# Value products of the third and fourth chunk in one run, and the scores around that run in another order

## Chip, core and metric

One NeuronCore of a Trainium2 chip runs the whole program. The metric is the device time of one execution in microseconds (us), as the median of several runs. A profile of one execution gives every instruction's start and duration.

## What is computed

A gate mixes sliding-window attention with a SwiGLU feed-forward network, for S = 2048 rows of D = 512 in fp32 (H = 32 heads of 16, window W = 256, F = 1792):

```python
def _A_ref(x, wqkv, wo):
    q, k, v = ...                       # x @ wqkv, H heads of 16
    scores = einsum("bhqd,bhkd->bhqk", q, k) * 16 ** -0.5
    p = softmax(where(0 <= q - k < 256, scores, -1e9))
    return einsum("bhqk,bhkd->bhqd", p, v)... @ wo
def _B_ref(x, w_gate, w_up, w_down):
    return (silu(x @ w_gate) * (x @ w_up)) @ w_down
g = sigmoid((x * gate_w).sum(-1, keepdims=True))
return g * _A_ref(x, ...) + (1 - g) * _B_ref(x, ...)
```

## The kernel before, in words

Products that need fp32 accuracy are made of two reduced-precision halves: each operand is split into a high and a low part (`split`), and three products are added.

The heads are worked on in eight groups of four (`g` = 0 to 7); the keys and queries in 16 blocks of 128 rows; the output of a group in four chunks of 512 queries (`c` = 0 to 3). The program has a start (projections of the first groups and all values), a main loop, and a last part (`with ExitStack() as B`: output projection and down projection).

The main loop runs over 128 slots `t` (and one more), 16 for each group; `i` is `t` modulo 16. The order of the instructions on every engine is that in which the Python code issues them; nothing is reordered by a planner. A slot has four turns (`hd`). In each turn TensorE gets:

- one score product of `stage1` for the next group (L263), into one of two `ps1` buffers of PSUM. VectorE (DVE) adds the mask and takes the row maximum from it (L265);
- one score product of `stage2` for this group (L305), into one of two `ps2` buffers. ScalarE (ACT) takes its exponential into a tile `pt` of SBUF (L307), and GpSimd (POOL) zeroes what lies outside the window (L309, L312). The two scores of a turn use the two halves of the array's rows (`j` is 0 or 1) and run at the same time;
- three pairs of matmuls of a projection or of the feed-forward network (`lanes`, L215), one matmul of a pair on each half of the rows, into `pa` or `pb` (two buffers each).

In the last group (slots from `g7` = 112) there is no `stage1`; the `stage2` scores come in pairs in turns 0 and 2, one pair in `ps2` and the other in `ps1`.

Value products (`av`, L329) multiply exponentials by values: 48 products for a chunk (32 for chunk 0), in 64x32 pieces of the array, each of them two instructions in fp32. They add into one `pp` buffer (`pb`, or `pa` for the very last chunk) and one `ps2` buffer. `values` issues them behind turn 1: chunks 0 and 1 of a group in one run in slot `i` = 8, chunk 2 in `i` = 12, chunk 3 in `i` = 0 of the next group. Then `finish` runs for each chunk, its steps spread over later turns by `times`: ACT copies the `ps2` part, DVE adds the other part, transposes (`across`), divides, transposes (`back`), and POOL sends the result to memory.

`unit` spreads the L215 work: four slots make one unit, and ACT copies its results out of `pa` and `pb` in slots that `later` names; `late` moves the two copies of the second half up to the end of the unit's last slot. `put_max` and `get_max` send the row maxima by memory into the query tiles; `load_v` fetches the values of four blocks into one of three `vg` buffers. After the loop, what is still in `FIN` and `AT` is issued. The last part begins with 24 products (L736), then the down projection (L83 to L85), whose operands come from ACT (L739, L65) and DVE (L740, L68).

Before all this, ten small matmuls on an identity tile (L175) keep TensorE busy while the first inputs arrive.

Of the kernel before, what the change touches and what calls it, by code (L numbers as in the profile page):

```python
# [9 lines left out]
F32 = mybir.dt.float32  # L10
F32R = mybir.dt.float32r
AF = mybir.ActivationFunctionType
ALU = mybir.AluOpType
# [3 lines left out]
P = 128  # L17
# [16 lines left out]
def gated_mix(ctx, tc, xT, xn, w01, wqk, wv, wo, wgu, wd, gw, out):  # L34
# [9 lines left out]

    ident = const.tile([P, P], F32, name="ident")
    make_identity(nc, ident)
    vd = dram.tile([G, P, NB, VW], F32, name="vd")
# [121 lines left out]
    with ExitStack() as A:  # L169
        sm = A.enter_context(tc.tile_pool(name="sm", bufs=2))  # L170


        warm = pp.tile([P, CH], F32, name="pa")
        for _ in range(5):
            nc.tensor.matmul(warm[:, :P], ident, ident, start=True, stop=True)  # L175

        mask = sm.tile([P, 3 * P], F32, name="mask", bufs=1)

        def kept():
            return sm.tile([P, CH], F32, name="ev", bufs=EV)  # L180

# [69 lines left out]
        def stage1(g, qb):  # L251

            hf, b = divmod(qb, NB // 2)
            if b == 0:
                MX[g, hf] = sm.tile([P, 4, NB // 2], F32, name="mx")
            q0, k0 = qb * P, max(0, qb - 2) * P
# [15 lines left out]
        def put_max(g, hf):  # L272
            mt = sm.tile([P, 32], F32, name="mt")
# [12 lines left out]
        VG, PT, AV = {}, {}, {}  # L286
        RC = sm.tile([P, CH // 32], F32, name="rc", bufs=1)

        def load_v(n):

            VG[n] = sm.tile([P, 4, VW], F32, name="vg", bufs=3)
            nc.sync.dma_start(VG[n], vd[n // 4, :, n % 4 * 4:n % 4 * 4 + 4])

        def stage2(g, kb):
# [4 lines left out]
            for hd in (1, 0, 3, 2):  # L299
                pr, j = divmod(hd, 2)  # L300
                r = slice(64 * j, 64 * j + 64)
                if j:
                    pt = PT[g, kb, pr] = ptp.tile([P, 2, 3 * P], F32, name="pt")
# [197 lines left out]
        for c in range(2, NCH):  # L501
            run(proj(1, c, pp, "pb"))
        stack(1, 1)
        for n in range(3):
            load_v(n)
        vp.close()
        osb = A.enter_context(tc.tile_pool(name="osb", bufs=3))
        ptp = A.enter_context(tc.tile_pool(name="ptp", bufs=17))

# [8 lines left out]
        def unit(key, t):  # L518
# [81 lines left out]
        def gate_done():  # L600
            nc.scalar.activation(gate, gate, AF.Exp, scale=-1.0)
            nc.vector.tensor_scalar(gate, gate, 1.0, None, op0=ALU.add)
            nc.vector.reciprocal(gate, gate)
            nc.vector.tensor_scalar(igate, gate, -1.0, 1.0, op0=ALU.mult, op1=ALU.add)
        later(g7 + NB - 1, 3, gate_done)

        FIN, tops = {}, [(0, 1)]
        LOADS = {9: 3, 13: 4, 17: 5, 18: 6}  # L610

        def values(t):

            ag, m = divmod(t - 8, NB)
            if m == 0:
                cs, times = (0, 1), [((0, 1),) * 2 + ((0, 3), (2, 0), (2, 3)), ((0, 1), (0, 2), (1, 1), (3, 2), (4, 1))]
            else:
                cs, times = (1 + m // 4,), [((0, 1), (0, 2), (1, 1), (2, 1), (3, 1))]
            for c in cs:
                av(ag, c)  # L620
            for k, steps in enumerate(zip(*(finish(ag, c) for c in cs))):
                for todo, ts in zip(steps, times):
                    dt, hd = ts[k]
                    if (dt, hd) == (0, 1):
                        todo()
                    else:
                        FIN.setdefault((t + dt, hd), []).append(todo)
        for t in range(G * NB + 1):
# [4 lines left out]
            s1 = stage1(g + 1, i) if t < g7 else iter(())  # L633
            s2 = stage2(g, i) if t < G * NB else iter(())
            for hd in range(4):
                run(s1, 1)
                if t < g7:
                    run(s2, 1)
                elif hd % 2 == 0:
                    run(s2, 2)  # L640
                run(turns[part], 3)
                for f in FIN.pop((t, hd), ()):
                    f()
                for f in AT.pop((t, hd), ()):
                    f()
                if hd == 1 and part == 0:
                    while tops:
                        top = tops.pop()
                        put_max(*top)
                        later(t + 1, 1, lambda top=top: get_max(*top))  # L650
# [10 lines left out]
        for key in sorted(AT):  # L661
            for f in AT[key]:
                f()

    with ExitStack() as B:
# [178 lines left out]
```

## Time and profile before

| what | value |
|---|---|
| time, median of 3 runs | 819.94 us (819.65 to 819.96) |
| the profiled execution's own time | 819.19 us |
| its span, first to last instruction | 817.2 us |
| TensorE (PE) busy | 810.5 us, 99% of the span |
| DVE / ACT / POOL busy | 513.5 / 452.9 / 343.4 us |

In the profile PE is a matmul, PEld a weight load, and L12 is line 12 of the kernel. `pb<-pt,vg` says that the tile `pb` is written from `pt` and `vg`; `ps` stands for the buffers `ps1` and `ps2`. The profiled execution is 0.75 us under the median of the runs.

### The profile page before, as it was taken

The page shows a single profiled execution, that of the slowest core. Times are in us where ns is not written, and L with a number is a line of the kernel's source. Part 1 is how long each engine was busy: PE and PEld are TensorE (multiplying, and loading weights), DVE is VectorE, ACT ScalarE, POOL GpSimd, SP SyncE. Part 2 cuts the span into 40 slices and gives each one's busy share as a digit, 9 for nine tenths or more (in the row PEclk, how much of TensorE's full clock was granted, in tenths as well). Part 3 has the DMA queues.
Part 4 walks back from the last instruction along what each step waited for, and adds up shares of the span by engine and source line. Part 5 has one row for each costly group of instructions (what it writes and reads, how often), then busy time and mean ns, then how long its engine had stood idle before and what let it go on. Part 6 is the DMA issues. An engine that isn't in the chain of part 4 may idle for free.

```text
span 817.2 us, 21557 instructions
## 1 busy us (share of the span) xinstructions
PE 810.5 (99%) x8306; PEld 681.7 (83%) x8306; DVE 513.5 (63%) x1422; ACT 452.9 (55%) x940; POOL 343.4 (42%) x635
## 2 busy tenths in 40 slices
PE   9999999999999999999999999999999999999997
PEld 5788988888888888898888888888788888888886
DVE  5596667667668667677677678854467443443542
ACT  6422656656666666676666665666666423343341
POOL 5812546645546555654554654465610111011020
PEclk9999999999999999999999999999999999999999
DMA  8484615625634642652652565565689444463731
GB/s 295 113 262 145 182 68 165 195 76 151 184 109 118 189 147 85 175 174 70 187 179 89 161 185 165 161 217 171 216 302 322 156 139 141 159 203 103 221 89 52
DMA packets 70326, 133.27 MB, mean 163 GB/s; under 512 B 14288, under 2 KB 19024, under 8 KB 70224
## 3 DMA queue, kind: packets, MB, share of 16 engines
q1 hardware_dynamic: 65936, 116.95, 46.3%
q0 software_dynamic: 4288, 14.95, 5.1%
q8 instruction: 65, 1.06, 0.6%
q14 instruction: 37, 0.30, 0.1%
HBM read 61.08 MB, written 45.61 MB: 131 GB/s over the span
## 4 chain that ended last, share of the span: by engine, by line
PE 95%; DMA 2%; POOL 1%; SPq 1%; DVE 0%; issue 0%; ACT 0%; ACTq 0%
PE pb L215 24%; PE pa L215 24%; PE ps L85 6%; PE ps L83 6%; PE ps L84 6%; PE ps L263 6%; PE pb L329 6%; PE ps L305 5%; PE ps L329 3%; PE pb L85 2%; PE pb L83 2%; PE pb L84 2%; PE pa L736 1%; PE pb L736 1%; PE pb L195 1%; DMA k<-xT 1%
## 5 line engine op out<-in xcount | busy, mean ns | idle before, releaser
L265 DVE CUSTOM_DVE_ANT_0 ps<-ps,mask 128x384 f32<-128x384 f32 (+2 forms) x512 | 273.1, 540 | 119.0 <-PE ps L263 68.7
L307 ACT ACTIVATE pt<-ps 128x384 f32<-128x384 f32 (+2 forms) x512 | 239.4, 476 | 117.9 <-PE ps L305 57.5
L309 POOL TENSOR_SCALAR_AFFINE_SELECT pt<-pt 128x256 f32<-128x256 f32 x256 | 109.1, 426 | 222.3 <-ACT pt L307 209.3
L305 PE MATMUL ps<-q,k 64*128 64x384 f32 (+2 forms) x512 | 159.7, 326 | 0.0
L263 PE MATMUL ps<-k,q 63*128 63x384 f32 (+2 forms) x512 | 157.9, 328 | 0.0
L215 PE MATMUL pb<-xhi,wh 64*128 64x512 f32 x512 | 110.9, 393 | 0.0
L215 PE MATMUL pa<-xhi,wh 64*128 64x512 f32 x512 | 110.7, 393 | 0.0
L215 PE MATMUL pb<-xhi,wl 64*128 64x512 f32 x512 | 109.8, 392 | 0.0
L215 PE MATMUL pb<-xlo,wh 64*128 64x512 f32 x512 | 109.8, 391 | 0.0
L215 PE MATMUL pa<-xlo,wh 64*128 64x512 f32 x512 | 109.3, 391 | 0.0
L215 PE MATMUL pa<-xhi,wl 64*128 64x512 f32 x512 | 109.1, 391 | 0.0
L263 PEld LDWEIGHTS ps<-k,q 63*128 63x128 f32 x512 | 88.8, 185 | 14.2 <-issue 4.0
L312 POOL TENSOR_SCALAR_AFFINE_SELECT pt<-pt 128x256 f32<-128x256 f32 x224 | 96.9, 433 | 0.0
L305 PEld LDWEIGHTS ps<-q,k 64*128 64x128 f32 x512 | 91.4, 185 | 5.9 <-issue 0.6
L329 PE MATMUL ps<-pt,vg 64*32 64x320 f32 (+4 forms) x1408 | 75.1, 346 | 0.0
L740 DVE TENSOR_TENSOR sg<-got,sg 128x512 f32<-128x512 f32 x50 | 43.7, 874 | 48.1 <-ACT sg L739 48.1
L329 PE MATMUL pb<-pt,vg 64*32 64x320 f32 (+3 forms) x1360 | 72.3, 350 | 0.1
L265 DVE DVE_READ_ACCUMULATOR2_ANT mx<- 128x1 f32 x512 | 72.2, 141 | 0.0
L329 PEld LDWEIGHTS pb<-pt,vg 64*32 64x32 f32 x1360 | 48.8, 106 | 20.8 <-ACT pt L307 5.8
L215 PEld LDWEIGHTS pb<-xhi,wh 64*128 64x128 f32 x512 | 55.8, 185 | 8.1 <-ACT ev L529 0.2
L215 PEld LDWEIGHTS pa<-xhi,wh 64*128 64x128 f32 x512 | 55.7, 185 | 7.5 <-ACT ev L529 0.6
L215 PEld LDWEIGHTS pb<-xhi,wl 64*128 64x128 f32 x512 | 55.8, 184 | 7.1
(163 smaller groups left out, 1555.6 us busy)
## 6 DMA issues: line engine op xcount, KB each, us to landing
raws<-ev SPq DMA_DIRECT2D x100, 256.0 KB
got<-raws SPq DMA_DIRECT2D x100, 256.0 KB
od<-on POOLq DMA_DIRECT2D x32, 256.0 KB, 2.6
raw<-wgu SPq DMA_DIRECT2D x28, 256.0 KB
q<-xhi SPq DMA_DIRECT2D x56, 128.0 KB
k<-xhi SPq DMA_DIRECT2D x56, 128.0 KB
vd<-vs POOLq DMA_DIRECT2D x8, 672.0 KB, 6.0
vg<-vd SPq DMA_DIRECT2D x32, 168.0 KB
```

What stands on the lines that cost most here:

```text
L83: nc.tensor.matmul(ps, lh, rh, start=start and i == 0, stop=False)
L84: nc.tensor.matmul(ps, lh, rl, start=False, stop=False)
L85: nc.tensor.matmul(ps, ll, rh, start=False, stop=stop and i == n - 1)
L215: mm = nc.tensor.matmul(ps[me], w[r], x[r], start=not second and i == 0, stop=bool(second) and i == n - 1)
L263: nc.tensor.matmul(ps[:, :n], QT[g % 2][pr][r, q0:q0 + P], KT[g % 2][pr][r, k0:k0 + n], start=True, stop=True)
L265: mx = nc.vector.tensor_tensor_reduce(out=ps[:, :n], in0=ps[:, :n], in1=mask[:, 3 * P - n:], scale=1.0, scalar=NEG, op0=ALU.add, op1=ALU.m ...
L305: nc.tensor.matmul(ps[:, :n], KT[g % 2][pr][r, k0:k0 + P], QT[g % 2][pr][r, k0:k0 + n], start=True, stop=True)
L307: BEHIND.append(nc.scalar.activation(pt[:, j, :n], ps[:, :n], AF.Exp, scale=SCALE))
L309: nc.gpsimd.affine_select(out=pt[:, :, :P], in_=pt[:, :, :P], pattern=[[0, 2], [1, P]], compare_op=ALU.is_ge, fill=0.0, base=0, channel_mu ...
L312: nc.gpsimd.affine_select(out=pt[:, :, 2 * P:], in_=pt[:, :, 2 * P:], pattern=[[0, 2], [-1, P]], compare_op=ALU.is_ge, fill=0.0, base=-1, ...
L329: nc.tensor.matmul(AV[g, c][h][32 * j:32 * j + 32, q0 - c * CH:q1 - c * CH], VG[4 * g + kb // 4][o, kb % 4, 17 * j:17 * j + 32], PT[g, kb, ...
L740: nc.vector.tensor_tensor(out=sg, in0=gu[1], in1=sg, op=ALU.mult)
```

## The change

Chunks 2 and 3 are multiplied together in slot `i` = 0 of the next group, so that a group has two runs of value products in place of three. For that, the exponentials of blocks 6 to 15 have to be kept until then: there are 18 `pt` tiles in place of 17, and block 15 (128 queries wide) uses the free columns of block 14's tiles. The first `stage2` score of the next group can be issued only behind the run. So in slots with `i` = 0 (but not in slot 0) the scores are issued in another order: two of `stage1` behind turn 0's L215 work, none in turn 1, one of `stage1` and one of `stage2` at the head of turns 2 and 3, and two of `stage2` behind turn 3's L215 work. The copies of the unit that ends in `i` = 15 are now `late`. The steps of `finish`, `load_v`, `put_max`, the computing of `igate` and some memory are moved. The warm-up uses a tile zeroed by DVE.

```diff
-    ident = const.tile([P, P], F32, name="ident")
-    make_identity(nc, ident)
...
-        warm = pp.tile([P, CH], F32, name="pa")
-        for _ in range(5):
-            nc.tensor.matmul(warm[:, :P], ident, ident, start=True, stop=True)
+        warm, zero = pp.tile([P, CH], F32, name="pa"), kept()[:, :P]
+        nc.vector.memset(zero, 0.0)
+        for _ in range(5):
+            nc.tensor.matmul(warm[:, :P], zero, zero, start=True, stop=True)
...
-        RC = sm.tile([P, CH // 32], F32, name="rc", bufs=1)
+        RC = igate
...
-                if j:
+                if kb == NB - 1:
+                    pt = PT[g, kb, pr] = PT[g, kb - 1, pr][:, :, 2 * P:]
+                elif j:
                     pt = PT[g, kb, pr] = ptp.tile([P, 2, 3 * P], F32, name="pt")
...
-        ptp = A.enter_context(tc.tile_pool(name="ptp", bufs=17))
+        ptp = A.enter_context(tc.tile_pool(name="ptp", bufs=18))
...
-                    late = hf and (t >= g7 or t % NB == 4)
+                    late = hf and (t >= g7 or t % 8 == 4)
...
-        LOADS = {9: 3, 13: 4, 17: 5, 18: 6}
+        LOADS = {9: 3, 17: 4, 18: 5, 19: 6}
         def values(t):
-            ag, m = divmod(t - 8, NB)
-            if m == 0:
-                cs, times = (0, 1), [((0, 1),) * 2 + ((0, 3), (2, 0), (2, 3)), ((0, 1), (0, 2), (1, 1), (3, 2), (4, 1))]
-            else:
-                cs, times = (1 + m // 4,), [((0, 1), (0, 2), (1, 1), (2, 1), (3, 1))]
+            ag, hf = divmod(t // 8 - 1, 2)
+            cs = 2 * hf, 2 * hf + 1
+            times = ((0, 1), (0, 1), (0, 3), (2, 1), (3, 1)), ((0, 1), (0, 2), (1, 1), (5, 1), (6, 1))
...
+            while part == 0 and tops:
+                top = tops.pop()
+                put_max(*top)
+                later(t + 1, 1, lambda top=top: get_max(*top))
             for hd in range(4):
-                run(s1, 1)
-                if t < g7:
+                if t and i == 0:
+                    if hd > 1:
+                        run(s1, 1)
+                        run(s2, 1)
+                elif t < g7:
+                    run(s1, 1)
                     run(s2, 1)
                 elif hd % 2 == 0:
                     run(s2, 2)
                 run(turns[part], 3)
+                if t and i == 0 and hd in (0, 3):
+                    run((s1, s1, s1, s2)[hd], 2)
...
-                if hd == 1 and part == 0:
-                    while tops:
-                        ...
-                    if t > 4 and i != 4:
-                        values(t)
+                if hd == 1 and t and t % 8 == 0:
+                    values(t)
...
-            m = (t - 3) % NB + 3
+            m = (t - 4) % NB + 4
...
+        nc.vector.tensor_scalar(igate, gate, -1.0, 1.0, op0=ALU.mult, op1=ALU.add)
...
-        wop.tile([P, 1536], F32, name="rest")
+        wop.tile([P, 448], F32, name="rest")
...
-    nc = bacc.Bacc("TRN2", target_bir_lowering=False, num_devices=1, dynamic_dma_scratch_size=4096)
+    nc = bacc.Bacc("TRN2", target_bir_lowering=False, num_devices=1, dynamic_dma_scratch_size=2048)
```

The line that computed `igate` in `gate_done` is gone from there, and the tiles `mx` and `mt` have one buffer in place of two.

## Rows read from the trace of the kernel before

**Rows 1.** The page: busy time of the engines, and the last chain by engine.

```profile
PE 810.5 (99%) x8306; PEld 681.7 (83%) x8306; DVE 513.5 (63%) x1422; ACT 452.9 (55%) x940; POOL 343.4 (42%) x635
...
PE 95%; DMA 2%; POOL 1%; SPq 1%; DVE 0%; issue 0%; ACT 0%; ACTq 0%
```

**Rows 2.** PE's waits: total us, times, longest us.

```profile
PE pa L175 <- POOL ident masks.py:199: 1.4, 1, 1.4
...
PE pa L195 <- DMA q<-xT: 0.2, 1, 0.2
```

**Rows 3.** Windows between the pair runs of neighbouring groups: length, then busy us.

```profile
108.82:173.79 64.97, 64.97 (x865) 55.39 (x864) 46.08 (x153) 42.21 (x93) 35.41 (x72) 1.00 0.46 143
...
433.70:498.67 64.97, 64.97 (x866) 55.40 (x864) 46.08 (x153) 42.20 (x93) 35.46 (x72) 1.00 0.53 159
```

**Rows 4.** Timeline of PE, one regular turn: start us, duration us.

```profile
380.01 0.33 PE L305 MATMUL ps<-q,k 64*128 64x384 f32 x1
380.18 0.39 PE L215 MATMUL pa<-xhi,wh 64*128 64x512 f32 x2
...
380.88 0.33 PE L305 MATMUL ps<-q,k 64*128 64x384 f32 x1
```

**Rows 5.** Timeline of ACT, the exponentials of that turn's and the next turn's score.

```profile
380.47 0.49 ACT L307 ACTIVATE pt<-ps 128x384 f32<-128x384 f32 x1 [0.43 <-PE ps L305]
381.29 0.49 ACT L307 ACTIVATE pt<-ps 128x384 f32<-128x384 f32 x1 [0.32 <-PE ps L263]
```

**Rows 6.** Timeline of PE around a run of one chunk (`i` = 12).

```profile
386.27 0.40 PE L215 MATMUL pa<-xhi,wh 64*128 64x512 f32 x2
...
387.07 0.45 PE L329 MATMUL pb<-pt,vg 64*32 64x320 f32 x1
...
389.04 0.27 PE L329 MATMUL pb<-pt,vg 64*32 64x128 f32 x1
...
389.55 0.44 PE L305 MATMUL ps<-q,k 64*128 64x384 f32 x1
389.83 0.40 PE L215 MATMUL pa<-xhi,wh 64*128 64x512 f32 x2
```

**Rows 7.** Timeline of PE in a run of chunks 0 and 1.

```profile
370.16 0.31 PE L329 MATMUL ps<-pt,vg 64*32 64x64 f32 x8
...
370.45 0.45 PE L329 MATMUL ps<-pt,vg 64*32 64x320 f32 x1
...
372.94 0.44 PE L305 MATMUL ps<-q,k 64*128 64x384 f32 x1
```

**Rows 8.** Timeline of ACT, its first copy behind that run.

```profile
373.04 0.59 ACT L342 COPY on<-ps 128x512 f32<-128x512 f32 x1 [1.72 <-PE ps L329]
```

**Rows 9.** Timeline of ACT in slot 112.

```profile
532.71 0.59 ACT L529 COPY ev<-pb 128x512 f32<-128x512 f32 x1
```

**Rows 10.** Timeline of PE in slot 112.

```profile
532.84 0.41 PE L215 MATMUL pa<-xhi,wl 64*128 64x512 f32 x2
533.36 0.45 PE L329 MATMUL pb<-pt,vg 64*32 64x320 f32 x1
```

**Rows 11.** Timeline of PE, the last run of the loop (slot 128).

```profile
592.29 0.45 PE L329 MATMUL pa<-pt,vg 64*32 64x320 f32 x1
```

**Rows 12.** Timeline of ACT at the end of the loop.

```profile
592.41 1.07 ACT L529 COPY ev<-pb 128x512 f32<-128x512 f32 x2 [0.36 <-PE pb L215]
```

**Rows 13.** Timeline of DVE in the first steps of the last part.

```profile
596.97 0.69 DVE L346 TENSOR_TENSOR on<-pa,on 128x512 f32<-128x512 f32 x1 [4.22 <-ACT on L342]
...
601.54 0.70 DVE L352 STREAM_TRANSPOSE on<-on 128x512 f32<-128x512 f32 x1
...
603.66 0.65 DVE L740 TENSOR_TENSOR sg<-pb,sg 128x512 f32<-128x512 f32 x1
...
605.00 0.69 DVE L68 TENSOR_TENSOR hl<-sg,hh 128x512 fp32r<-128x512 f32 x1
```

**Rows 14.** Timeline of PE where the last part first uses that product.

```profile
606.24 0.39 PE L85 MATMUL ps<-k,hl 128*128 128x512 f32 x1
```

More of the change, by code (lines that the diff above doesn't have):

```diff
@@ L7 @@
 from concourse._compat import with_exitstack
-from concourse.masks import make_identity
 F32 = mybir.dt.float32
@@ L170, in gated_mix @@
         sm = A.enter_context(tc.tile_pool(name="sm", bufs=2))
-        warm = pp.tile([P, CH], F32, name="pa")
-        for _ in range(5):
-            nc.tensor.matmul(warm[:, :P], ident, ident, start=True, stop=True)
-        mask = sm.tile([P, 3 * P], F32, name="mask", bufs=1)
         def kept():
             return sm.tile([P, CH], F32, name="ev", bufs=EV)
+        warm, zero = pp.tile([P, CH], F32, name="pa"), kept()[:, :P]
+        nc.vector.memset(zero, 0.0)
+        for _ in range(5):
+            nc.tensor.matmul(warm[:, :P], zero, zero, start=True, stop=True)
+        mask = sm.tile([P, 3 * P], F32, name="mask", bufs=1)
         X = {}
@@ L254, in stage1 @@
             if b == 0:
-                MX[g, hf] = sm.tile([P, 4, NB // 2], F32, name="mx")
+                MX[g, hf] = (sm if g or hf else vpool).tile([P, 4, NB // 2], F32, name="mx", bufs=1)
             q0, k0 = qb * P, max(0, qb - 2) * P
@@ L272, in put_max @@
         def put_max(g, hf):
-            mt = sm.tile([P, 32], F32, name="mt")
+            mt = sm.tile([P, 32], F32, name="mt", bufs=1)
             nc.vector.transpose(mt, MX[g, hf].rearrange("p h b -> p (h b)"))
@@ L286, in gated_mix @@
         VG, PT, AV = {}, {}, {}
-        RC = sm.tile([P, CH // 32], F32, name="rc", bufs=1)
+        RC = igate
         def load_v(n):
-            VG[n] = sm.tile([P, 4, VW], F32, name="vg", bufs=3)
+            VG[n] = vgp.tile([P, 4, VW], F32, name="vg", bufs=3)
             nc.sync.dma_start(VG[n], vd[n // 4, :, n % 4 * 4:n % 4 * 4 + 4])
@@ L503, in gated_mix @@
         stack(1, 1)
+        vp.close()
+        osb = A.enter_context(tc.tile_pool(name="osb", bufs=3))
+        ptp = A.enter_context(tc.tile_pool(name="ptp", bufs=18))
+        vgp = A.enter_context(tc.tile_pool(name="vgp", bufs=3))
         for n in range(3):
             load_v(n)
-        vp.close()
-        osb = A.enter_context(tc.tile_pool(name="osb", bufs=3))
-        ptp = A.enter_context(tc.tile_pool(name="ptp", bufs=17))
         AT = {}
@@ L603, in gate_done @@
             nc.vector.reciprocal(gate, gate)
-            nc.vector.tensor_scalar(igate, gate, -1.0, 1.0, op0=ALU.mult, op1=ALU.add)
         later(g7 + NB - 1, 3, gate_done)
         FIN, tops = {}, [(0, 1)]
-        LOADS = {9: 3, 13: 4, 17: 5, 18: 6}
+        LOADS = {9: 3, 17: 4, 18: 5, 19: 6}
         def values(t):
-            ag, m = divmod(t - 8, NB)
-            if m == 0:
-                cs, times = (0, 1), [((0, 1),) * 2 + ((0, 3), (2, 0), (2, 3)), ((0, 1), (0, 2), (1, 1), (3, 2), (4, 1))]
-            else:
-                cs, times = (1 + m // 4,), [((0, 1), (0, 2), (1, 1), (2, 1), (3, 1))]
+            ag, hf = divmod(t // 8 - 1, 2)
+            cs = 2 * hf, 2 * hf + 1
+            times = ((0, 1), (0, 1), (0, 3), (2, 1), (3, 1)), ((0, 1), (0, 2), (1, 1), (5, 1), (6, 1))
             for c in cs:
@@ L645, in gated_mix @@
                     f()
-                if hd == 1 and part == 0:
-                    while tops:
-                        top = tops.pop()
-                        put_max(*top)
-                        later(t + 1, 1, lambda top=top: get_max(*top))
-                    if t > 4 and i != 4:
-                        values(t)
+                if hd == 1 and t and t % 8 == 0:
+                    values(t)
             if i in (7, 15) and g + 1 < G:
                 tops.append((g + 1, i // 8))
-            m = (t - 3) % NB + 3
+            m = (t - 4) % NB + 4
             if t > 8 and m in LOADS and (t - m) // 4 + LOADS[m] < 4 * G:
```

## Prediction

> **What bounds the kernel.** I read the page's busy times and its last chain first. TensorE is busy for 810.5 of the 817.2 us, and 95% of the chain that ended last is TensorE's [rows 1]. The reader is to see that no other engine comes near: DVE has 63%, ACT 55%. So I asked next what TensorE itself waits for. The list of its waits has three entries and less than 2 us, all at the start [rows 2], where the first and the last stand. There is almost no idle time to win. A change can only win if TensorE's own work becomes shorter, and it loses every wait that it adds, in full.
>
> Then I looked at windows of one group each. All six from the first pair run at 108.82 to 498.67 last 64.97 to 64.98 us, with TensorE busy throughout [rows 3], where the first and the last stand. The main loop is therefore a steady beat, and what one group gains or loses can be multiplied. Last, I read timelines: TensorE in a regular turn, around a run of one chunk, inside a pair run; ACT behind such runs; and the seam to the last part.
>
> A regular turn is two scores side by side, 0.17 us (380.01 to 380.18), and three pairs of L215, 0.70 us (to 380.88) [rows 4]: 0.87 us.
>
> **What a run of value products costs beyond its columns.** The L215 stretch ahead of a run lasts 0.80 us (386.27 to 387.07) in place of 0.70: +0.10. The scores behind it last 0.28 us (389.55 to 389.83) in place of 0.17: +0.11 [rows 4, 6]. And the run's own last step takes 0.51 us when a score follows (389.04 to 389.55) but 0.29 us when the next chunk follows (370.16 to 370.45) [rows 6, 7]. Chunk 0's last step is half as wide on one half of the rows, so part of this 0.22 us is width; for two full chunks I take 0.15, with 0 and 0.22 as bounds. A run less saves 0.10 + 0.11 + 0.15 = 0.36 us, bounds 0.21 and 0.43. Eight pairs of runs are merged: behind groups 0 to 6 in slots 16 to 112, and behind group 7 in slot 128. For the first seven that is 7 x 0.36 = -2.5 us.
>
> In slot 112 the old run also waits for ACT's copy out of `pb`: it starts 0.52 us after the last L215 pair (532.84 to 533.36), where 0.34 us is normal (0.80 of rows 6 less two pairs of 0.23, a third of 0.70), and ACT's copy ends at 533.30 [rows 6, 9, 10]. The copies are now issued a turn or more earlier, so this goes: -0.2 us.
>
> **What the new order of scores adds.** There are two `ps2` buffers. A `stage2` score can be written into one only when the exponential of the score two places earlier has been read out of it. In a regular turn the distance between those is two turns, 1.74 us. What it must be at least, I add up: the exponential starts 0.46 us after its score (380.01 to 380.47) and lasts 0.49 [rows 4, 5], and TensorE goes on 0.06 us after ACT's end (533.30 to 533.36) [rows 9, 10]: 1.01 us. In the next turn the exponential starts 0.41 us after its score (380.88 to 381.29) [rows 4, 5]; that gives 0.96.
>
> In slots with `i` = 0 the third and fourth `stage2` scores now stand behind turn 3's L215 work, and the fifth, of the next slot, right behind them. Between the third and the fifth, which share a buffer, TensorE has only one pair of scores, 0.17 us [rows 4]. So the fifth waits 0.79 to 0.84 us; I take 0.80. Queued behind it on TensorE are the L215 pairs of the next turn and everything after; nothing else gives TensorE work. The lower bound is 0, if TensorE could go on past it (a rival, below); the upper is 0.95, with the 0.11 us of a restart [rows 4, 6] on top. The first and second score do not wait: they need the `ps2` buffers of the run, whose second copy starts 0.10 us after the run and lasts 0.59 [rows 7, 8], within a turn. In slots 16 to 96 that makes six waits, 6 x 0.80 = +4.8 us. In slot 112 there is none, because two of the four scores go to `ps1` in the last group.
>
> What remains of the order costs nothing: the same scores with the same columns go to each half of the rows. `stage1`'s two scores in a row find both `ps1` buffers read, since 0.70 us of L215 work now stands ahead of them. The bounds are one restart, 0.11 us, either way in each of six slots, so 0.7.
>
> **The end of the loop.** In slot 128 no L215 work stands ahead of the run, and chunk 2 goes into `pb`, where chunk 3 alone went into `pa`. The last unit's `pb` copies start at 592.41 and take 1.07 us for both [rows 12]; one of 0.59 [rows 9] is over at 593.00, and 0.06 later the run can start: 593.06, where it started at 592.29 [rows 11]. That is +0.77, less the 0.36 of the merged run: +0.4 us.
>
> Behind it, DVE has two chunks to finish rather than one. A chunk's transposes and division take 2.1 us (601.54 to 603.66). The sum with ACT's copy came 2.1 us after the run's end at 594.85 (596.97) because ACT had other work first; the new run ends 3.0 us later, so 1.4 us of that go, as a copy and a wait still take 0.7. With 0.17 us for `igate`, the product at 603.66 comes 0.9 us later against TensorE. Its low half ends at 605.69, and TensorE wants it at 606.24 [rows 13, 14]: 0.55 us cover, so +0.3 us, at most 1.7 if ACT's time isn't gained back.
>
> **Edits that I cost at nothing.** The warm-up may start some tenths earlier, but real work starts when the first input arrives [rows 2]; if the identity's loss shortened everything by its whole wait, it would be 1.4 us. `load_v`, `put_max` and the moved `finish` steps go to SP, DVE and POOL, which have slots to spare (DVE 63% busy [rows 1]); their values are used four slots later or more. If that cover were gone, they would show as waits of L329 or L305. Block 15's exponentials go into columns that nobody else writes. `late` puts two copies of 0.59 us [rows 9] ahead of slot 0, where ACT now has no exponential to do. The addresses and the smaller DMA scratch move no work.
>
> **Sum.** -2.5 - 0.2 + 4.8 + 0.4 + 0.3 = +2.8 us. On the profiled execution's own 819.19 that is 822.0; the median of the runs stands 0.75 higher, so **822.7 us**.
>
> **Rivals.** One: TensorE goes on past the waiting score with the L215 pairs behind it, and the six waits cost nothing. Then -2.5 - 0.2 + 0.4 + 0.3 = -2.0: **817.9 us**, faster. It decides when a wait costs under 2.0 / 6 = 0.33 us. For it speaks that weight loads do run ahead; against it, that in slot 112 nothing ran in the 0.18 us in which L329 waited [rows 10]. The Trainium skill, "TensorE: Matmul & The Clock Gate", "The mechanism" in Part 3, says that matmuls start and end strictly in order and that only weight loads are pulled ahead; by that rule this rival falls and the waits count in full, and the trace agrees with its 0.18 us.
>
> Two: the merged runs save more. If a full chunk ahead of another costs by columns what chunk 0 does (1.73 us for 4/5 of the columns, so 2.16 in place of 2.48), a merge saves 0.32 + 0.21 = 0.53 us, 8 x 0.17 = 1.4 us more: **821.3 us**, no measurable change. For it: chunk 0's short last step [rows 7]. Against: that step is narrow.
>
> Three: DVE becomes the bound at the seam for as long as a second chunk takes, and the restart adds its 0.11 us six times: +1.4 and +0.7, **824.8 us**. Against it: DVE's 0.55 us cover and the gain at ACT.
>
> **Chances.** Forecast 0.66, rival one 0.12, two 0.14, three 0.08. The forecast's own range is 821.4 to 824.0, by the bounds of 0.36 and 0.80. The range 820.0 to 824.6 leaves out rival one and part of three. A measurement of this kernel tells about 0.2%, 1.6 us, from no change. Faster: rival one and a little, 0.13; the same: most of two and the forecast's lower edge, 0.16; slower: 0.71.
>
> **What would show it.** In the new profile, a group should last about 65.4 us rather than 64.97. Each of slots 17, 33, ... 97 should begin with an idle TensorE of some 0.8 us, released by ACT's L307. The longer steps ahead of and behind a run should appear twice per group, and a run of two full chunks should last 4.82 us. At the loop's end L329 should wait for ACT's L529. I am wrong if the waits of L305 on L307 are missing or well under 0.33 us, or if they appear and TensorE's stretches elsewhere shrink by as much.

## The result and the profile after

The changed kernel takes 831.34 us (median of 4 runs, 829.71 to 832.77); the kernel before, on the same chip, 819.91. The ratio is 1.0139, with an interval of 1.012 to 1.0158: slower by 11.4 us. The forecast was 822.7 with a range up to 824.6. The forecast had the sign right, and a quarter of the size.

The profiled execution lasts 831.56 us. This is its page: the span, the busy time of the engines, and the last chain by engine and by line.

```profile
span 829.9 us, 21530 instructions
...
PE 814.4 (98%) x8306; PEld 707.4 (85%) x8306; DVE 518.9 (63%) x1423; ACT 456.3 (55%) x940; POOL 344.9 (42%) x633
...
PE 90%; DMA 3%; POOL 3%; issue 2%; ACT 1%; DVE 0%; SPq 0%; POOLq 0%; ACTq 0%
PE pb L213 23%; PE pa L213 22%; PE ps L82 6%; PE ps L80 6%; PE ps L81 6%; PE ps L261 5%; PE pb L329 5%; PE ps L305 5%; PE ps L329 4%; PE pb L82 2%; PE pb L81 2%; PE pb L80 2%; PE pa L740 1%; PE pb L740 1%; DMA vd<-vs 1%
```

Against [rows 1], TensorE has fallen from 95% to 90% of the chain. GpSimd has risen from 1% to 3%, "issue" (time in which an engine waits for nothing that the profile shows) from 0 to 2%, ACT from 0 to 1%, and the transfer `vd<-vs` is new among its lines. TensorE's list of waits, in total us, times and longest us, was short and lay at the start [rows 2]. Now it reads:

```profile
PE ps L305 <- ACT pt L307: 3.5, 7, 1.6
PE pb L329 <- issue: 1.4, 1, 1.4
PE pa L213 <- issue: 1.4, 1, 1.4
...
PE pb L329 <- ACT ev L530: 1.0, 2, 0.7
PE ps L261 <- DVE mx L263: 0.7, 1, 0.7
PE pa L213 <- ACT vs L407: 0.7, 1, 0.7
```

The first line is the wait that I forecast, six times, and once 1.6 us at the first exponentials. The rest, but for L530, I had not forecast. The 12.7 us by which the span grew lie in three places.

**Ahead of the loop: 4.0 us.** The first run of value products starts at 112.82; before, at 108.82 [rows 3]. Two stops, 50.94 to 52.02 and 83.11 to 84.96, make most of it. Another 0.7 us is lost before 33 us, as the same product starts at 32.62 in place of 31.92; the granted clock had risen at 7.58 in place of 5.00 (the warm-up, below). GpSimd's waits between 30 and 113 us show what is late:

```profile
POOL vd L402 <- issue: 19.5, 4, 5.5
```

In the kernel before the same view of the same stretch has

```profile
POOL vd L402 <- ACT vs L407: 28.8, 6, 8.8
```

Before, six of the eight sends of `vd` waited for the copy that fills their buffer. Now four of them stand on the queue with nothing missing that the profile shows, up to 5.5 us, which is what the page gives from the issue of such a send to its landing. The chain of work that ended last shows the order of events around the first stop (start, length):

```profile
40.17 5.54 issue
45.71 5.59 DMA vd<-vs
...
51.38 0.59 ACT vs L407
51.98 0.04 issue
52.02 2.55 PE pa L213 x10
```

The second send is issued at 45.71, and the trace has the landing of the first at 45.40. So it goes on: each of the seven later sends is issued 0.30 or 0.31 us after the one before it has landed. In the kernel before, the first two follow each other at once, though the first lands only at 45.09:

```profile
38.43 1.96 POOL L402 DMA_DIRECT2D vd<-vs  x2
```

**In six groups: 5.3 us.** Windows between neighbouring pair runs, longest and shortest of six (64.97 or 64.98 each before [rows 3]):

```profile
178.84:245.25 66.41, 65.52 (x865) 58.72 (x865) 47.16 (x152) 42.78 (x93) 35.91 (x72) 1.00 0.46 140
245.25:310.86 65.61, 65.29 (x865) 58.87 (x864) 47.05 (x152) 42.67 (x93) 35.91 (x72) 1.00 0.47 142
```

The forecast was 65.4. The wait behind the run is in every group. TensorE in slot 64, from the start of turn 1 to that of turn 2, with the run between, and from the start of turn 3 into slot 65:

```profile
342.19 0.46 PE L213 MATMUL pa<-xhi,wh 64*128 64x512 f32 x2
...
347.95 0.51 PE L213 MATMUL pa<-xhi,wh 64*128 64x512 f32 x2
...
348.83 0.44 PE L213 MATMUL pa<-xhi,wh 64*128 64x512 f32 x2
...
349.57 0.49 PE L305 MATMUL ps<-q,k 64*128 64x384 f32 x2
349.90 0.28 PE L261 MATMUL ps<-k,q 63*128 63x256 f32 x1
350.49 0.44 PE L305 MATMUL ps<-q,k 64*128 64x384 f32 x1 [0.31 <-ACT pt L307]
350.49 0.67 PE L213 MATMUL pb<-xhi,wh 64*128 64x512 f32 x2
```

The same turn 1 in the kernel before, with the run of one chunk:

```profile
337.53 0.44 PE L215 MATMUL pa<-xhi,wh 64*128 64x512 f32 x2
...
341.00 0.45 PE L215 MATMUL pa<-xhi,wh 64*128 64x512 f32 x1
```

A second loss stands in slot 13 of each group, where chunk 1's divide now lies. DVE and GpSimd in slot 29:

```profile
200.83 1.01 DVE L357 TENSOR_TENSOR on<-on,igate 128x256 f32<-128x256 f32 x1
201.76 0.55 DVE L263 CUSTOM_DVE_ANT_0 ps<-ps,mask 128x384 f32<-128x384 f32 x1
```

```profile
200.27 1.29 POOL L65 TENSOR_TENSOR wl<-raw,wh 128x512 fp32r<-128x512 f32 x1
```

This multiply of DVE takes 0.42 us at its shortest. Here it meets GpSimd's subtraction, takes 1.01 (0.99 to 1.02 in the six groups), and L263 behind it starts late. Turn 3 of slot 13 is 0.23 us longer than before in each group.

**Behind 507.96: 3.4 us.** Here stand the two lines "issue" of TensorE's waits, a wait in slot 108 (527.71 to 528.82, L261 behind DVE), and the wait in slot 128 that I forecast. TensorE in slot 120, in the middle of a run, and then in slot 128:

```profile
576.55 0.27 PE L329 MATMUL ps<-pt,vg 64*32 64x128 f32 x1
578.27 0.27 PE L329 MATMUL pb<-pt,vg 64*32 64x128 f32 x1 [1.45 <-issue]
...
601.63 0.61 PE L213 MATMUL pb<-xhi,wl 64*128 64x512 f32 x2
602.91 0.45 PE L329 MATMUL pb<-pt,vg 64*32 64x320 f32 x1 [0.68 <-ACT ev L530]
```

The stop at 576.55 follows no work of another engine. The stretch from 574 to 579 us has, in the view of the DMA queues (packets, MB, share), besides data,

```profile
q8 instruction: 1, 0.02, 3.1%
```

That is one packet of 16 KB of instructions; its record runs from 574.45 to 576.91, and TensorE goes on 1.36 us after its end. Two more stops look the same: 215.62 to 216.48 (slot 32, 1.47 us after a packet's end) and 545.29 to 547.23 (slot 112, 1.28). All three lie in, or just behind, runs of 160 or 192 short matmuls with as many weight loads. The profile puts most of the one in slot 32 down to ACT's L342, a copy that starts at 215.72 there. In slot 64, though, the same score starts at 347.79, ahead of that copy (347.92), so it doesn't need it.

### The profile page after: what moved, and what is told of

Its sections match the earlier page's. It is cut to its first block, busy times and chain, and to the rows that moved or that the text cites. A ratio compares the mean times of both kernels' runs of the same rounds, so it can differ in the third digit from the quotient of the medians.

```text
span 829.9 us, 21530 instructions
## 1 busy us (share of the span) xinstructions
PE 814.4 (98%) x8306; PEld 707.4 (85%) x8306; DVE 518.9 (63%) x1423; ACT 456.3 (55%) x940; POOL 344.9 (42%) x633
## 3 DMA queue, kind: packets, MB, share of 16 engines
q8 instruction: 65, 1.06, 0.5%
## 4 chain that ended last, share of the span: by engine, by line
PE 90%; DMA 3%; POOL 3%; issue 2%; ACT 1%; DVE 0%; SPq 0%; POOLq 0%; ACTq 0%
PE pb L213 23%; PE pa L213 22%; PE ps L82 6%; PE ps L80 6%; PE ps L81 6%; PE ps L261 5%; PE pb L329 5%; PE ps L305 5%; PE ps L329 4%; PE pb L82 2%; PE pb L81 2%; PE pb L80 2%; PE pa L740 1%; PE pb L740 1%; DMA vd<-vs 1%
## 5 line engine op out<-in xcount | busy, mean ns | idle before, releaser
L263 DVE CUSTOM_DVE_ANT_0 ps<-ps,mask 128x384 f32<-128x384 f32 (+2 forms) x512 | 272.0, 541 | 100.7 <-PE ps L261 74.9
L307 ACT ACTIVATE pt<-ps 128x384 f32<-128x384 f32 (+2 forms) x512 | 238.9, 477 | 125.2 <-PE ps L305 63.9
L261 PE MATMUL ps<-k,q 63*128 63x384 f32 (+2 forms) x512 | 161.7, 328 | 0.7 <-DVE mx L263 0.7
L305 PE MATMUL ps<-q,k 64*128 64x384 f32 (+2 forms) x512 | 158.1, 328 | 4.0 <-ACT pt L307 3.5
L213 PE MATMUL pb<-xhi,wh 64*128 64x512 f32 x512 | 117.4, 394 | 0.0
L213 PE MATMUL pa<-xhi,wh 64*128 64x512 f32 x512 | 115.5, 394 | 1.4 <-issue 1.4
L213 PE MATMUL pb<-xhi,wl 64*128 64x512 f32 x512 | 115.6, 392 | 0.0
L213 PE MATMUL pb<-xlo,wh 64*128 64x512 f32 x512 | 115.5, 391 | 0.0
L213 PE MATMUL pa<-xlo,wh 64*128 64x512 f32 x512 | 114.2, 391 | 0.0
L213 PE MATMUL pa<-xhi,wl 64*128 64x512 f32 x512 | 114.1, 391 | 0.0
L261 PEld LDWEIGHTS ps<-k,q 63*128 63x128 f32 x512 | 91.4, 185 | 14.2 <-DVE mx L263 3.5
L305 PEld LDWEIGHTS ps<-q,k 64*128 64x128 f32 x512 | 90.9, 185 | 7.7 <-ACT pt L307 5.3
L263 DVE DVE_READ_ACCUMULATOR2_ANT mx<- 128x1 f32 x512 | 71.7, 140 | 0.0
L213 PEld LDWEIGHTS pb<-xhi,wh 64*128 64x128 f32 x512 | 62.4, 185 | 4.6
L213 PEld LDWEIGHTS pb<-xhi,wl 64*128 64x128 f32 x512 | 62.3, 184 | 4.4
L213 PEld LDWEIGHTS pa<-xhi,wh 64*128 64x128 f32 x512 | 61.1, 185 | 4.8 <-issue 0.7
```

What stands on the lines that cost most here:

```text
L213: mm = nc.tensor.matmul(ps[me], w[r], x[r], start=not second and i == 0, stop=bool(second) and i == n - 1)
L261: nc.tensor.matmul(ps[:, :n], QT[g % 2][pr][r, q0:q0 + P], KT[g % 2][pr][r, k0:k0 + n], start=True, stop=True)
L263: mx = nc.vector.tensor_tensor_reduce(out=ps[:, :n], in0=ps[:, :n], in1=mask[:, 3 * P - n:], scale=1.0, scalar=NEG, op0=ALU.add, op1=ALU.m ...
L305: nc.tensor.matmul(ps[:, :n], KT[g % 2][pr][r, k0:k0 + P], QT[g % 2][pr][r, k0:k0 + n], start=True, stop=True)
L307: BEHIND.append(nc.scalar.activation(pt[:, j, :n], ps[:, :n], AF.Exp, scale=SCALE))
```

## The experiments

"Against before" is the difference of the medians on one chip, and the ratio with its interval; the changed kernel stands at +11.4.

| run | us | against before |
|---|---|---|
| e1 before, small DMA memory | 822.60 | +3.0, 1.0041 [1.0027, 1.0056] |
| e2 before, zeros in the warm-up | 820.42 | +0.8, 1.0011 [1.0002, 1.0021] |
| e3 after, old order of scores | 828.34 | +8.8, 1.0104 [1.0089, 1.0119] |
| e4 after, every other send on SyncE | 831.42 | +11.8, 1.0143 [1.0112, 1.0174] |
| e5 after, old turns for chunks 0, 1 | 827.51 | +7.9, 1.0098 [1.0085, 1.0112] |
| e6 after, three runs split | 830.53 | +10.9, 1.0132 [1.0118, 1.0146] |
| e7 after, sends on ScalarE | 828.70 | +9.1, 1.0106 [1.0092, 1.012] |
| e8 four edits | 822.41 | +2.8, 1.0034 [1.0022, 1.0046] |
| e9 e8, gate's blocks later | 820.44 | +0.6, 1.0005 [0.9996, 1.0014] |
| e10 e9, two runs split | 821.47 | +1.6, 1.0017 [1.0008, 1.0026] |
| e11 e10, identity | 821.76 | +1.9, 1.0021 [1.0011, 1.003] |
| e12 e9, packets shifted | 819.23 | -0.6, 0.999 [0.9982, 0.9999] |
| e13 e12, down weights later | 818.27 | -1.6, 0.9984 [0.9975, 0.9993] |
| e14 before, shifted | 819.77 | -0.1, 0.9999 [0.9991, 1.0008] |
| e15 after, shifted | 827.51 | +7.7, 1.0103 [1.0087, 1.0118] |

**The DMA memory and the sends (e1, e4, e7).** e1 makes only this edit in the kernel before:

```diff
-... dynamic_dma_scratch_size=4096)
+... dynamic_dma_scratch_size=2048)
```

> The kernel before with one edit: the memory for descriptors of POOL's transfers is halved (4096 to 2048). Theory A: with the half, POOL can't issue a vd<-vs send before the one ahead of it has landed (in the changed kernel POOL sat before L402 for 19.5 us in 4 waits, none in the kernel before), so ACT's copies into vs and POOL's own splits come late, and TensorE loses about 1.2 us at 50 us and 2.1 us at 84 us: 819.9 + 3.3 = 823.2 us. Rival: the size costs nothing, and the 4.0 us by which the changed kernel's main loop starts late come from the warm-up and from where the tiles lie: 819.9 us, no wait of POOL before L402.

It costs 3.0 us. GpSimd's waits between 30 and 113 us now begin, in the kernel before too, with

```profile
POOL vd L402 <- issue: 22.4, 5, 5.6
```

So the size is what holds the sends: six of the seven later ones are issued 0.30 to 0.32 us after the landing of the one before. e4 sends half of them on SyncE:

```diff
-nc.gpsimd.dma_start(vd[:, :, b - 1:b + 1]...
+(nc.sync if b % 4 == 3 else nc.gpsimd).dma_start(vd[:, :, b - 1:b + 1]...
```

> The changed kernel, with every other vd<-vs send issued by SP in place of POOL; the small scratch stays. Theory A (the sends wait for each other on POOL): POOL's waits before L402 shrink from 19.5 us to under 5, TensorE's losses at 50 and 84 us go, the main loop starts 3 us earlier: 831.3 - 3.3 = 828.0 us. Rival: the start is late for the warm-up or for the tiles' places, or SP's queue is held up by the sends instead: 831 us or more.

Its runs spread from 828.2 to 834.8, so the times decide nothing. The three longer ones have a mean granted clock of 0.997 or 0.998, the shortest 1.0. In its trace, of the shortest, the stop at 84 us is gone and the one at 51 us stays. e7 puts all of them on ScalarE:

```diff
-nc.gpsimd.dma_start(vd[:, :, b - 1:b + 1]...
+nc.scalar.dma_start(vd[:, :, b - 1:b + 1]...
```

> The kernel after, with all the sends of vd issued by ScalarE, right behind the copy that fills the buffer, and none by GpSimd. Theory A: it was the halved memory for GpSimd's descriptors that held each send back until the one before had gone, and so the buffers that the next copies fill; with the sends on another queue both stalls of the first projections (1.2 us at 51 and 2.1 us at 83) go, the first run of value products starts about 110 instead of 112.8, and the time is about 828.5. Rival: the sends are slow by themselves (the stalls come back on ScalarE's queue, with ScalarE behind them): 831 or more.

It gains 2.4 us by the medians, and in its profiled execution the first run starts at 109.12, 0.3 us from the kernel before. ACT's timeline, the two copies and the send behind them, shows what a send costs there (0.37 to 0.54 us in all eight; GpSimd took 0.89 to 1.06):

```profile
44.39 1.08 ACT L407 COPY vs<-pb 128x512 f32<-128x512 f32 x2 [8.11 <-PE pb L213]
45.50 0.37 ACTq L402 DMA_DIRECT2D vd<-vs  x1
```

The Trainium skill, "DMA: Bandwidth & Descriptors", section "SWDGE vs HWDGE vs iDMA", says that GpSimd writes the descriptors of its transfers into rings in SBUF, and that transfers issued by SyncE or ScalarE don't use these. e1 and e7 agree with it: halving the memory costs 3.0 us, and leaving that path returns 2.4.

**The warm-up (e2).**

```diff
-    make_identity(nc, ident)
+    nc.vector.memset(ident, 0.0)
```

> The kernel before with the warm-up matmuls on a tile that DVE sets to zero, in place of the identity that POOL makes. In the changed kernel the granted clock was full only from 7.6 us of the span, in the kernel before from 5.0 us, and the first projections were 1.0 us late by 15 us, 0.7 us by 33 us. Theory A: the warm-up's data or its earlier end holds the clock at its lower level for longer: +0.7 us, 820.6 us, and the clock rises after 7 us again. Rival: that is chance from one execution to the next, or it comes from the first inputs: 819.9 us and the clock rises at about 5 us.

The +0.8 us fits, and in its profile the granted clock rises from the lower level, 1.2 GHz, to 2.4 at 9.16 us, against 5.00 before (up to there the first projection's products start 0.86 us apart, behind it 0.43). But e1, with the identity, rose at 7.49. e11, below, tells more.

**The order of scores (e3).**

```diff
-                if t and i == 0 and hd in (0, 3):
-                    run((s1, s1, s1, s2)[hd], 2)
+                if t and i == 0 and hd != 1:
+                    run(s2 if hd else s1, 1 if hd else 2)
```

> The changed kernel with the stage2 scores of a slot with i = 0 spread: one at the head and one at the end of turns 2 and 3, in place of two at the end of turn 3. Theory A (the prediction's wait): the fifth score no longer stands 0.17 us behind the third but about 0.95 us, the wait of 0.6 us and its slow restart of 0.1 us go in all six groups, and 0.1 to 0.2 us of smaller waits stay: 831.3 - 3.3 = 828.0 us, between 827.5 and 829.5. Rival: the waits are not what the time hangs on (ACT's exponentials are, or another wait comes in their place): 831 us.

The waits of L305 on L307 are gone from the groups, and the kernel gains 2.7 us, 0.45 a group. Its profiled execution, the longest of the four, also shows what a stop can bring with it: TensorE stood from 82.98 to 85.11, and from 85.85 to 89.26 its granted clock was at the lower level,

```profile
85.85:89.26 3.41, 3.41 (x20) 3.41 (x19) 0.85 (x4) 1.71 (x4) 2.49 (x5) 0.50 0.77 201
```

with pairs of L213 starting 0.42 us apart in place of 0.23. That cost it 1.6 us more.

**The finish steps (e5).**

```diff
+            if not hf:
+                times = ((0, 1), (0, 1), (0, 3), (2, 0), (2, 3)), ((0, 1), (0, 2), (1, 1), (3, 2), (4, 1))
```

> The kernel after, with the finish steps of chunks 0 and 1 at the turns of the kernel before (chunk 0's at (2,0) and (2,3), chunk 1's divide and back at (3,2) and (4,1)); chunks 2 and 3 keep theirs. Theory A: chunk 1's divide met GpSimd's split of the projections and its multiply lasted 1.0 us in place of 0.43, so that a first-stage score waited for VectorE in slot 13 of each group (+0.23 us a group) and once at slot 108 (1.1 us). The multiply is back at 0.43, both waits go, and the time is about 829 (-0.23 x 7 - 0.8). Rival: the divide meets other work at the old turn too, or the score then waits for the next thing in VectorE's row, and the time stays 831.

It gains 3.6 us, more than the 2.4 expected. The wait in slot 13 goes. The one in slot 108 does not: it grows to 1.67 us, since chunk 1's last transpose is back in that slot. What makes up the difference is not settled. By the trace the steps themselves are worth 0.23 us in each of six groups, 1.4 in all, less 0.6 in slot 108. In this execution the first run also starts 1.3 us earlier (111.55), the stop of slot 32 is missing (0.9 us), and the one of slot 120 is 0.6 in place of 1.7; no run ties these to the steps, and e4 and e7, which leave the steps alone, lack the stop of slot 32 too. A group is now this long:

```profile
242.53:307.90 65.37, 65.05 (x865) 58.75 (x865) 46.59 (x152) 42.62 (x93) 35.39 (x72) 1.00 0.46 142
```

**Three runs split (e6).**

```diff
             for c in cs:
+                if c == cs[1] and t in (32, 112, 120):
+                    run(turns[part], 3)
                 av(ag, c)
```

> The kernel after, with one turn of projection products (the next turn's) put between the two chunks of the runs in slots 32, 112 and 120, the three at which TensorE stopped though nothing that the profile shows was missing. Theory A: in these runs of 384 short matmuls TensorE uses its instructions up faster than the next 16 KB of them arrive, so slower products in between let the fetch catch up: the stops of 0.9, 1.7 and 1.3 us go, three drains of about 0.3 are added, and the time is about 828.5. Rival: the stops have another cause and stay, or move to other runs; the time is 831 to 832.

In the trace the stops of slots 32 and 120 are gone, and that of slot 112 has shrunk from 1.9 us to 0.7 and moved into the second half of the run. The time falls by only 0.5 us, less than the interval: the three added drains, and in this execution a wait for a copy in slot 96 (473.94 to 474.76), take it back. The trace leans to theory A, but not by much: e4, without a split, has no long stop in slots 32 and 120 either. The time leaves it open.

**Four edits together (e8).** e3, e5 and e7, and chunk 2 of the last run in the other tile:

```diff
-name="pb" if 4 * g + c + 1 < len(UNITS) else "pa"),
+name="pb" if 4 * g + c + 2 != len(UNITS) else "pa"),
```

> The kernel after with four things together: scores of the slot after a group's end in the order of before, finish steps of chunks 0 and 1 at the turns of before, sends of vd on ScalarE, and chunk 2 of the last run in the other tile, so that nothing waits for the copies of slot 128. Theory A (each cost is its own and they add): 831.3 - 3.0 - 2.2 - 2.8 - 0.75 = about 822.5, what is left over the kernel before being the stops of TensorE in or just behind runs of two chunks, some 3 us, and the warm-up, 0.8, less the merges. Rival: the costs hide each other (the engine that waited here waits elsewhere), and the time is 825 or more.

822.41 against 822.5 expected: within some 1 us of noise the costs are separate and add. A late group lasts

```profile
369.33:434.20 64.87, 64.87 (x866) 58.73 (x865) 46.59 (x152) 42.57 (x93) 35.52 (x72) 1.00 0.47 143
```

0.1 us less than before. What was left: stops in slots 112 and 120 (1.3 and 1.0 us), and slot 108. DVE there:

```profile
517.32 0.71 DVE L362 STREAM_TRANSPOSE on<-on 128x512 f32<-128x512 f32 x1
517.95 0.90 DVE L563 SCALAR_TENSOR_TENSOR xhi<-xlo,xhi 128x512 f32<-128x512 f32 x1
518.78 0.08 DVE L563 DVE_READ_ACCUMULATOR xhi<-xlo,xhi 128x1 f32 x1
518.78 0.42 DVE L64 CAST q<-ev 128x512 fp32r<-128x512 f32 x1
519.23 0.69 DVE L65 TENSOR_TENSOR q<-ev,q 128x512 fp32r<-128x512 f32 x1
519.84 0.56 DVE L263 CUSTOM_DVE_ANT_0 ps<-ps,mask 128x384 f32<-128x384 f32 x1
```

From 517.3 to 519.8 DVE has no time for a score's maximum, and TensorE stands from 518.83 to 520.51. The kernel before has the same steps in this slot, but also this, on TensorE:

```profile
517.01 0.45 PE L329 MATMUL pb<-pt,vg 64*32 64x320 f32 x1
```

It is the first matmul of a single run, 2.5 us in which TensorE wants nothing of DVE. The merge moved this run to slot 112, and with it the cover.

**Slot 108 and the stops (e9 to e12).** e9 moves the gate's blocks out:

```diff
-... enumerate([(-8, 1), (-8, 1), (-4, 1)] + [(t, 3) for t in range(-2, NB - 5)]):
+... enumerate([(-8, 1), (-8, 1)] + [(t, 3) for t in range(0, NB - 2)]):
```

> The kernel with the four edits, and with the gate's block products 2 to 15 of VectorE (0.90 us for one) begun at slot 112 in place of 108, one a slot. Theory A: in slot 108 VectorE has 5.7 us of work for a slot of 3.5, and in the kernel before the run of a single chunk that stood in this slot gave it 2.5 us to catch up; the merge took that cover away, and a score waits 1.7 us. With 0.98 us less in the slot most of the wait goes: -1.0 to -1.7, 820.7 to 821.4. Rival: the wait comes from the split of the down weights (1.1 us) alone and stays, or the later blocks make a new one: 822.4 or more.

2.2 us gained, more than expected, and no difference left to the kernel before. The gap in slot 108 falls from 1.67 to 1.06, and the stop of slot 112 (1.3) is missing too. Whether that is the changed pace ahead of it or the gate's transfers, which moved along, was not tried. e10 splits the two runs left with stops (the edit of e6 with `t in (112, 120)`):

> The kernel of the run before in this list, with one turn of projection products between the two chunks of the runs in slots 112 and 120. Theory A: the two stops of TensorE that are left there (1.3 and 1.0 us) are its instructions coming too late in or behind 320 and 384 short matmuls without a pause; with the pause they shrink to under 0.5 each, at 0.3 a drain: about 1.0 us below the run before, 819.5 to 820.5. Rival: the stops stay, or come back elsewhere, and the time is that of the run before or up to 0.6 above.

A miss: the gain didn't come, and the median is 1.0 us higher, about as much as the noise. The long gaps go from its trace, but the drains and the slots behind them cost as much or more. e11 adds the identity to it:

```diff
-        nc.vector.memset(zero, 0.0)
+        make_identity(nc, zero)
```

> The same with two runs split, and with the identity in the place of the zeros in the five products of the start. Theory A (from the kernel before with zeros, +0.8): 0.8 below, about 819. Rival: the granted clock rises when it does whatever the operands hold; the time is that of the run before, within 0.3.

No gain: the rival holds. The clock rose at 8.09 us here and at 6.29 in e10 with zeros. TensorE has the same instructions in e10 and e11, and yet e11's trace has a stop again, of 1.1 us in the second part of slot 120's split run (569.37 to 570.49, 1.47 us after a packet's end). So a split doesn't keep them off, and the stops also differ between executions. e12 takes e9 and shifts what follows on TensorE by some 108 instructions:

```diff
-        for _ in range(5):
-            nc.tensor.matmul(warm[:, :P], zero, zero, start=True, stop=True)
+        for _ in range(32):
+            nc.tensor.matmul(warm[:32, :32], zero[:, :32], zero[:, :32], start=True, stop=True)
```

> The kernel with the gate's blocks later and no run split; at the start 32 products of 32 columns stand in place of 5 of 128, which puts some 108 more instructions ahead of everything on TensorE and shifts where the packets of 16 KB of instructions begin. Theory A: the stops depend on where in a run the next packet is fetched, so that those of slots 112 and 120 change size or go, and others may come in other runs; the time moves by up to 2.5 us either way with the sum of the stops. Rival: the stops belong to the slots (work of other engines) and stay at 1.3 and 1.0 us.

1.2 us gained by the medians. The stop inside slot 120's run, which e9 still had (0.8), is gone, and slot 112 has 0.3 us. New ones stand at 340.64 (slot 64, 0.65 us, resumed 1.45 after a packet's end) and 504.94 (0.52, 1.42). The stops have changed places; the two profiled executions themselves last the same (819.95 and 819.92 us), so the trace doesn't show where the 1.2 us come from.

**Control, the changed kernel itself, and a better version (e13 to e15).** e14 and e15 make e12's edit alone in the kernel before (with `ident`) and in the changed one:

> The kernel before, with 32 products of 32 columns in place of its 5 of 128 at the start. A control: theory A (what the shift gained in the last list, 1.2 us, was the stops of TensorE behind the merged runs, of which the kernel before has hardly any): no change, 819.8 within 0.5. Rival (the gain was a shorter or better start): about 1 us below, 818.7.

> The kernel after with nothing else changed than those products at the start. Theory A (the stops in slots 32, 112 and 120, 3.9 us in the profiled execution, depend on where the packets of instructions begin against the runs): they go or change places, and the time falls by 1 to 3 us to 828 to 830. Rival (they belong to what the slots do): the same three stops, 831.3 within 1.

Before stays where it was; the changed kernel gains 3.8 us. All three stops are gone from its trace; slots 112 and 120 are 3.5 us shorter than in the trace of the changed kernel. The one of slot 32 tells little, as it is missing without a shift in e4, e5 and e7 too. In slots 112 and 120 the contrast is wide: without the shift and without a split, the changed kernel, e3, e4, e5, e7 and e8 all stop in slot 112 (0.9 to 1.9 us), and all of these but e4 in slot 120 (0.6 to 1.7), e9 in slot 120 alone, while none of the three shifted kernels has a stop of that size there. One of 0.5 us is new, in slot 64 (344.19, resumed 1.36 us after a packet's end), where e12 had its own. e13 takes e12 and moves the split of slot 108:

```diff
-... enumerate(((-8, 1), (-4, 1), (0, 1), (2, 2)...
+... enumerate(((-8, 1), (12, 2), (0, 1), (2, 2)...
```

> The shifted kernel of the last list with one more step moved: the split of the down weights that stands in slot 108 goes to slot 124, where VectorE is idle. Theory A (the rest of the wait in slot 108, 1.0 us, is VectorE's row there): the wait goes, 819.2 - 0.9 = 818.3, and this is below the kernel before by 0.2%. Rival: ScalarE's or GpSimd's part of the split delays the copies of slot 124 and the seam, and the time stays 819.2 or rises.

818.27 us, 1.6 below the kernel before: the fastest here. The other edits in it would hardly help the kernel before: it has no wait that they could remove (its list of waits is under 2 us, all at the start [rows 2]), and the shift alone gave it nothing (e14). TensorE's list of waits is down to

```profile
PE pa L176 <- DVE ev L174: 1.1, 1, 1.1
PE ps L261 <- issue: 0.4, 1, 0.4
PE pa L193 <- DVE xlo L65: 0.3, 1, 0.3
```

## Why the prediction fell short, step by step

What failed are four things that the sum put at nothing. The terms that it did price came out close to the forecast.

- **"The addresses and the smaller DMA scratch move no work" failed.** It was a judgement without a row. Alone the smaller memory costs 3.0 us (e1). With half of it GpSimd's queue issued a send of `vd`, its largest, only after the one before had landed, and held each for up to 5.6 us; that held the copy into its buffer, and this TensorE.
- **"The moved finish steps go to SP, DVE and POOL, which have slots to spare (DVE 63% busy)" failed**, by an average over stages. The divide was moved onto GpSimd's split, 0.42 us became 1.01, and the score behind it came late, +0.23 us a group, 1.4 in six; with the old turns this is gone (e5). The Trainium skill, "SBUF — State Buffer", section "Who interferes with whom", has a rule for it: a VectorE instruction with two inputs in SBUF and a GpSimd instruction that reads SBUF exclude each other, and the second waits. By full exclusion the multiply would end 0.73 + 0.42 = 1.15 us after its start (201.56 less 200.83, and its own time); the trace has 1.01. GpSimd's spans are rough, so the trace fits the rule without showing it exactly. I had read this trace for durations, not for what runs beside what.
- **The merge's price left out its cover.** I counted what a run less saves, not what the run hid. In slot 108 it hid 2.5 us of DVE; without it TensorE stops there for 1.1 us. e13 shows it: with that slot cleared the wait is gone from the trace, and the median falls by 1.0 us. Part of e9's 2.2 is the same.
- **The merge's price left out TensorE's instructions.** The 13 stops of this kind in the traces of the changed kernel, e3, e8, e12, e13 and e15 all end 1.3 to 1.6 us after the end of a packet of 16 KB on the instruction queue; the kernel before, e1, e2 and e14, without merged runs, have none. Shifting the stream removes or moves them (e12, e15), while the kernel before gains nothing by it (e14). In the changed kernel this is worth 3.5 us by the traces and 3.8 by the medians. That the long run of short matmuls empties what TensorE has in store is the reading that fits; it isn't shown, and how far ahead it fetches was not measured.
- **The new order of scores cost what was forecast.** 0.80 us a group was the term. Turn 3 of slot 64 with the scores behind it takes 1.66 us (348.83 to 350.49), a regular turn 0.87 [rows 4]: +0.79. Of this, 0.59 us is the way from L261 to the fifth score. The next turn is 0.13 longer, a restart, and turn 0 as much shorter, so a group pays 0.79. Undoing the order returns only 0.45 to 0.51 of it (e3; e8's 64.87 against e5's 65.37), because e3's order itself costs 0.3 over that of before. Rival one is refuted: TensorE stood still.
- **The merge saved what was forecast.** Slot 12's turn falls from 3.56 us (386.27 to 389.83 [rows 6]) to 0.88, and slot 0's turn 1 grows from 3.47 (337.53 to 341.00) to 5.76 (342.19 to 347.95): 2.68 less 2.29, or 0.39 us saved, in place of 0.36. A run of two full chunks, first matmul to next score, lasts 4.74 us; 4.82 was forecast. Rival two, 0.53 us, is not borne out. So the group with the finish steps restored lasts 65.37 where the two terms give 65.41, and neither of them is right by luck. What is left in a group is small: slot 8 pays 0.07 to 0.1, which was not followed further, and slot 15 gives 0.06.
- **Slot 128 was right:** TensorE waits there for L530, 0.75 us longer than in a usual step (0.77 forecast). In slot 112 the copy wait is gone, as forecast. DVE at the seam, +0.3, did not come: from the first product of the last part to the end it is 222.20 us, against 222.38.
- **The warm-up** is open. e2 says +0.8 us, e11 says no gain from undoing it. It is at most a small part.
- **The forecast's own range** does not follow from the bounds that it names. 0.21 and 0.43 in place of 0.36 move eight merges by -0.6 to +1.2 us, 822.1 to 823.9; 0 and 0.95 in place of 0.80 move six waits by -4.8 to +0.9.

By the two profiled executions, the 12.7 us of the span add up so. Ahead of the loop: 4.0. In six groups: 4.8 for the order of scores, 1.4 for slot 13, 0.6 for slot 8, and 1.3 for a late copy and a stop at the runs of slots 16 and 32, less 2.8 for the merges and slot 15; that is 5.3. Behind them: 1.0 in slot 108, 3.5 for the stops of slots 112 and 120, and 0.75 in slot 128, less 1.9 for the rest, mostly the last merges; that is 3.4. The gains of single experiments (2.4, 2.7, 3.6, 3.8) can't be added like this: they are medians of four executions that lie 2 to 4 us apart, and in the profiled ones of e5 and e15 the first run starts 1.3 and 2.3 us earlier than in the changed kernel's, which neither edit was meant to do.

## What to carry to other kernels

When work is merged or moved on the engine that sets the time, list what it covered on the other engines in that slot, by name and microseconds; a busy share over the whole kernel says nothing about it. An edit that looks like bookkeeping (here the size of a buffer for descriptors, 3.0 us) needs a row of its own, or its price is unknown. And a useful merge can lie under its side effects: cleared of most of them, the new order of scores among them, it was 1.6 us faster than before instead of 11.4 slower.

## What the runs showed of the hardware

- With half the memory for descriptors, GpSimd's sends of 672 KB were issued 0.3 us after the landing of the one before (seven of seven in the changed kernel, six of seven in e1), 4.5 to 7 us apart; with the full memory two went out 1.1 us apart. ScalarE issued the same send in 0.37 to 0.54 us, GpSimd in 0.89 to 1.06.
- TensorE stopped for 0.5 to 1.9 us with nothing missing that the profile shows, each time going on 1.3 to 1.6 us after the end of a packet of 16 KB of its instructions, mostly in or behind runs of 160 to 192 short matmuls with their weight loads. 108 instructions more at the start of the kernel moved the stops to other slots.
- The granted clock rose to its upper level between 4.2 us (e14) and 9.2 us (e2) after the start, with the same operands at different times in different executions. In e3 it fell to the lower level for 3.4 us after TensorE had stood for 2.1; after a stop of 1.85 us in the changed kernel it didn't.
